# Inverse 47-point DFT of a long convolution: three overlapping products per eight values of m in place of five separate ones

## The chip, the cores and the metric

One core of a Trainium2 chip runs the whole kernel in one launch. The metric is the device time of one execution in microseconds. The kernel before was timed three times; every table below comes from those times and from one further execution that was profiled.

## The reference

The input x has 8 batches of 3008 positions and 256 channels. Each channel of each batch is filtered in the frequency domain, and every resulting position then goes through a two-layer network with a rational activation:

```python
X = np.fft.rfft(x, axis=1)
Y = X * (filt_r + 1j * filt_i)[None, :, :]
y = np.fft.irfft(Y, n=3008, axis=1)            # 8 x 3008 x 256
h = y.reshape(24064, 256) @ w_in               # 2048 columns
P = a[0] + a[1]*h + a[2]*h**2 + a[3]*h**3
Q = 1.0 + np.abs(b[0])*np.abs(h) + np.abs(b[1])*h**2
out = (P / (Q + 1e-6)) @ w_out                 # 24064 x 256
```

## The kernel before

The transform of length 3008 is split as 64 x 47 (a prime-factor split, so that there are no twiddle factors between the two). It has three stages, all on TensorE (PE) in fp32.

*Stage 1* (`stage1`, lines 292 to 306) is the 47-point forward DFT: tiles of 96 rows (48 positions, one of them zero, times two halves of the 64) and 512 columns. A tile is loaded (`stage1_load`), multiplied by `a1_sb` on line 300, copied out by ACT (line 263, through `evac`) and stored to the DRAM scratch `scr1`.

*Stage 2* (`Stage2`, lines 308 to 389) reads `scr1` back with 128 rows (real and imaginary parts of 64 values), does the 64-point forward DFT (line 348), the product with the filter (lines 355, 356, 367, 372), and the 64-point inverse DFT (line 381), and stores the result to the scratch `scr2` (`store`, line 389). The result has one row of `scr2` for each of 24 frequencies k of the 47-point transform (the input is real, so 24 of 47 do), by 128 rows (real or imaginary part r, and m from 0 to 63), by 256 channels.

*Stage 3* (`stage3`, lines 410 to 438) is the inverse 47-point DFT, and turns channels onto partitions for the network. For one pair of values of m (m and m + 32) the data are 96 rows (24 k, two parts r, two halves) by 256 channels. The data are the stationary operand, 128 channels (one half `cc`) at a time, and the constant `e_sb`, 96 x 94, is the moving one: 94 columns are the 47 positions of each of the two m. The 256 pairs are cut into 52 `chunks` of five (the first two are five and one). A chunk is one load `tl` (lines 419 and 420; the first two chunks in two row ranges), and for each `cc` five products side by side in one PSUM bank (line 426). ACT then copies the bank to `xh` as fp32r (line 435), and VectorE (DVE) writes the remainder to `xl` (line 437). `xh` and `xl` are rings of 1536 columns (`RX`), so that a piece across the end of the ring is written in two. In the profile, an fp32 product is two records of weight load (PEld) and matmul (PE); an fp32r product is one.

*The network* works on tiles of 512 positions, 47 in all, each in 16 `Unit`s of 128 hidden columns. A unit has six products into `h_u` (lines 459, 460, 462), a dozen elementwise operations on ACT, DVE and GpSimd (POOL), and six products into the two output banks (lines 536 to 538), issued `LAG` = 4 units later.

*The order.* The instruction order on PE, ACT, DVE and POOL is the order in which the program issues them. `first_batch` (the head, lines 595 to 646) does stages 1 and 2 of batch 0 and the first two chunks of stage 3, beside the unpacking of the weights. `pipeline` (lines 648 to 744) then runs the 752 units, and puts at most one item of convolution work into a unit: either one group of stage 3 (one `cc` of a chunk, two groups to a chunk) or one product of stages 1 and 2 of a later batch (`conv_items`), the latter against a credit of 0.38 per unit. A chunk is begun, with its load, in units 1 and 9 of a tile (`XF`), if the ring has room and the next tile needs it or its batch is ready (lines 689 to 700). All loads and stores of this stage are issued by the SP queue, in order of the program; a load into a buffer waits on SP until its last readers are done. `tl` has two buffers, so chunk k waits for the products of chunk k - 2.

Of the kernel before, what the change touches and what calls it, by code (L numbers as in the profile page):

```python
# [9 lines left out]
F32 = mybir.dt.float32  # L10
# [12 lines left out]
S = 3008  # L23
N1, N2 = 64, 47
NH = 32
K2 = 24
R1 = 96
C = 256
G = 94
GE = 96  # L30
DFF = 2048
LAG = 4
RATES = 0.6, 0.38
# [26 lines left out]
def shape_constants():  # L60
    n2 = np.arange(N2)
    k2 = np.arange(K2)
    th = 2 * np.pi * np.outer(n2, k2) / N2
    a1 = np.zeros((48, 2, K2, 2, 2))
    for h in range(2):
        a1[:N2, h, :, 0, h] = np.cos(th)
        a1[:N2, h, :, 1, h] = -np.sin(th)
    a1 = a1.reshape(R1, R1)

    ph = 2 * np.pi * np.outer(np.arange(N1), np.arange(N1)) / N1  # L70
    co, si = np.cos(ph), np.sin(ph)
    fwd = np.block([[co, -si], [si, co]])
    inv = np.block([[co, si], [-si, co]])

    e = np.zeros((K2, 2, 2, 2, N2))
    w = np.where(k2 == 0, 1.0, 2.0) / S
    for h in range(2):
        e[:, 0, h, h, :] = w[:, None] * np.cos(th.T)
        e[:, 1, h, h, :] = -w[:, None] * np.sin(th.T)
    e = e.reshape(R1, G)  # L80

    k = (N2 * np.arange(N1)[:, None] + N1 * k2[None, :]) % S
    sgn = np.where(k > S // 2, -1.0, 1.0)
    sgn[(k == 0) | (k == S // 2)] = 0.0
    sgn = np.concatenate([sgn, -sgn], 0)
    mats = np.zeros((128, 3, 128))
    mats[:, 0], mats[:, 1], mats[:, 2] = fwd, inv, np.concatenate([inv[64:], inv[:64]])
    small = np.zeros((R1, R1 + GE))
    small[:, :R1], small[:, R1 : R1 + G] = a1, e
    f = lambda v: np.ascontiguousarray(v, dtype=np.float32)  # L90
    return f(mats), f(small), f(sgn)


def index_maps():
# [5 lines left out]


@with_exitstack
def conv_moe(ctx: ExitStack, tc: tile.TileContext, xp, fr, fi, w_in, w_out, ab, mats, small, sgn, outT):
    nc = tc.nc
    B = xp.shape[0]

    consts = ctx.enter_context(tc.tile_pool(name="consts", bufs=1))
    dram = ctx.enter_context(tc.tile_pool(name="dram", bufs=3, space=DRAM))
    conv = ctx.enter_context(tc.tile_pool(name="conv", bufs=2))
# [8 lines left out]
    wo_sb = consts.tile([128, 8, 2, TT], F32R, name="wo_sb")  # L118
    xh = xl = None
    mats_sb = consts.tile([128, 3, 128], F32, name="mats_sb")  # L120
    small_sb = consts.tile([R1, R1 + GE], F32, name="small_sb")
    a1_sb, e_sb = small_sb[:, :R1], small_sb[:, R1 : R1 + G]
    words = consts.tile([128, 128], F32, name="words_sb")
    sgn_sb, ab_sb, abs_sb, cf_sb = words[:, :K2], words[:, 32:44], words[:, 64:76], words[:, 96:120]
    flag_sb = words[:, 120:121].bitcast(I32)
# [3 lines left out]
    col = lambda i, n=1: cf_sb[:, i : i + n]  # L129
# [5 lines left out]
    def load_flag():  # L135


        nc.scalar.activation(abs_sb, ab_sb, AF.Abs)
        sq, c, d, e = col(8, 2), col(10, 2), col(12, 2), col(14)
        tt(out=sq, in0=ab_sb[:, 6:8], in1=ab_sb[:, 6:8], op=ALU.mult)  # L140
        tt(out=c, in0=abs_sb[:, 8:10], in1=abs_sb[:, 10:12], op=ALU.mult)
        stt(out=c, in0=c, scalar=16.0, in1=sq, op0=ALU.mult, op1=ALU.is_ge)
        stt(out=c, in0=abs_sb[:, 10:12], scalar=1e-6, in1=c, op0=ALU.is_ge, op1=ALU.mult)
        stt(out=d, in0=abs_sb[:, 10:12], scalar=2e-6, in1=abs_sb[:, 6:8], op0=ALU.mult, op1=ALU.is_le)
        tt(out=c, in0=c, in1=d, op=ALU.mult)

        stt(out=e, in0=B1, scalar=4.000004, in1=col(9), op0=ALU.mult, op1=ALU.subtract)
        tt(out=e, in0=e, in1=e, op=ALU.mult)
        tt(out=col(9), in0=col(9), in1=col(9), op=ALU.mult)
        stt(out=e, in0=col(9), scalar=1e-10, in1=e, op0=ALU.mult, op1=ALU.is_le)  # L150
        tt(out=col(10), in0=col(10), in1=e, op=ALU.mult)
        tt(out=flag_sb, in0=col(10), in1=col(11), op=ALU.mult)
# [100 lines left out]
        return wo_sb[:, f // 2, k, c : c + 128]  # L253

    scr1 = [dram.tile([K2, 128, C], F32, tag="scr1", name=f"scr1_{b}") for b in range(B)]
    scr2 = [dram.tile([K2, 128, C], F32, tag="scr2", name=f"scr2_{b}") for b in range(B)]

    def rows(scr):
        return scr.rearrange("k (g m) c -> (k g) m c", m=NH)
# [23 lines left out]
    def stage1_load(b, q):  # L283

        tag = "xin" if b or q < XB else ("f1", "f2")[q % 2]
        xin = conv.tile([R1, 2, TT], F32, tag=tag, name=f"xin{b}_{q}", bufs=XB if tag == "xin" else FB)
        nc.sync.dma_start(
            xin.rearrange("p a b -> p (a b)"), xp[b, :, 4 * q : 4 * q + 4, :].rearrange("p m c -> p (m c)")
        )
        return xin  # L290
# [17 lines left out]
    class Stage2:  # L308
# [77 lines left out]
            banks.done(bank, 0.5)  # L386

        def store(self, q):
            nc.sync.dma_start(scr2[self.b][4 * q : 4 * q + 4].rearrange("k p c -> p k c"), self.ev.pop(q))

    def stage2(b):
        s = Stage2(b)
# [12 lines left out]
                s.store(i // 2 - 1)  # L405


    chunks = [(0, 5), (5, 6)] + [(g, min(g + 5, B * NH)) for g in range(6, B * NH, 5)]

    def stage3(k):  # L410

        g0, g1 = chunks[k]
        tl = conv.tile([R1, 5, C], F32, tag="tl", name=f"tl{k}")
        i = g0
        while i < g1:
            b, m = divmod(i, NH)
            n = min(g1, (b + 1) * NH) - i

            for r in (slice(0, 80), slice(80, R1)) if k < 2 else (slice(0, R1),):
                nc.sync.dma_start(tl[r, i - g0 : i - g0 + n], rows(scr2[b])[r, m : m + n, :])  # L420
            i += n
        for cc in range(2):
            yield 1.1
            bank, pt = banks.tile(f"x_{k}_{cc}")
            for i in range(g1 - g0):
                nc.tensor.matmul(  # L426
                    pt[:, i * G : i * G + G], tl[:, i, cc * 128 : cc * 128 + 128], e_sb, start=True, stop=True
                )
            yield

            t0, t1 = g0 * G, g1 * G
            cut = min(t1, (t0 // RX + 1) * RX)
            parts = [(slice(a % RX, a % RX + z - a), pt[:, a - t0 : z - t0]) for a, z in ((t0, cut), (cut, t1)) if a < z]
            for o, p in parts:
                nc.scalar.activation(xh[:, cc, o], p, AF.Copy)
            for o, p in parts:
                v.tensor_tensor(out=xl[:, cc, o], in0=p, in1=xh[:, cc, o].bitcast(F32), op=ALU.subtract)  # L437
            banks.done(bank, 0.5)
# [156 lines left out]
    def first_batch():  # L595

        s = Stage2(0)
        s.more = [xpool.tile([128, 6 - FB, 4, C], F32, tag=x, name=f"f{x}") for x in ("xh", "xl")]
        xin = {}
        fl = iter(range(6))  # L600

        def do(tokens):
            for c in tokens:
                if c == "W":
                    dec.load()
                elif c == "D":
                    dec.step()
                elif c == "F":
                    s.load_filter(next(fl))

        nc.scalar.dma_start(ab_sb, ab.rearrange("(o n) -> o n", o=1).broadcast_to([128, 12]))
        nc.sync.dma_start(small_sb, small)
        for q in range(8):
            xin[q] = stage1_load(0, q)
        do("W")
        nc.scalar.dma_start(sgn_sb, sgn)
        nc.scalar.dma_start(mats_sb, mats)
        load_flag()
        square_scalars()
        for q in range(8):  # L620
            run(stage1(0, q, xin.pop(q)))
            do(HA[q])
        for q in range(XB - 1):
            s.load(q)
        for q in range(2):
            s.double_filter(q)
        do(HM)
        for i in range(12 + ZL):
            if i < 12:
                run(s.product(i))  # L630
            if i >= ZL:
                run(s.inverse(i - ZL))
            q, j = divmod(i, 2)
            if j == 0 and q + XB - 1 < 6:
                s.load(q + XB - 1)
            elif j and q + 2 < 6:
                s.double_filter(q + 2)
            if i > ZL and (i - ZL) % 2:
                s.store((i - ZL) // 2)
            do(HB[i])  # L640
        nonlocal xh, xl
        xh, xl = (xpool.tile([128, 2, RX], F32R, tag=x, name=x) for x in ("xh", "xl"))
        for k in range(2):
            run(stage3(k))
        dec.part(HD)
        assert dec.done == dec.loaded == HD
# [134 lines left out]
def unpermute(outT, nb):  # L781
    seq, _ = index_maps()
    col = np.zeros(S, np.int64)
    col[seq.reshape(2, NH, N2).transpose(1, 0, 2).reshape(-1)] = np.arange(S)
    o = outT.reshape(C, nb, S)[:, :, col]
    return np.ascontiguousarray(o.transpose(1, 2, 0)).reshape(nb * S, C)

# [30 lines left out]
```

## Time and profile before

| what | value |
|---|---|
| median of three runs | 2540.5 us (2538.84 to 2540.68) |
| the profiled execution | 2541.1 us, span 2538.9 us |
| granted TensorE clock, mean | 0.988 |
| PE busy | 2483.7 us (98%) |
| DVE, ACT, POOL busy | 2263.7, 2199.2, 1856.3 us |
| stage 3 on PE, line 426 | 1024 records, 131.5 us busy |
| stage 3 evacuation | 134 instructions each on ACT (59.8 us busy) and DVE (68.2 us) |
| DMA | 208.76 MB, mean 82 GB/s |

The span is the time from the first to the last instruction of the profiled execution; its own time is 2.2 us longer. Records of matmuls overlap, and their ends are modelled, so a group's busy time is the union of its records and not their number times their mean. The time that a record really takes from PE is the distance between the starts of neighbours. A row of the chain of waits gives a start, a length, and the work that occupied that part of the chain; "x10" is ten records in a row.

### The profile page before, as it was taken

Reading aid. Unit: us, or ns where it says so; the run is one execution under the profiler, and the core shown is the slowest. Engines: PE = TensorE matmul, PEld = TensorE weight load, DVE = VectorE, ACT = ScalarE, POOL = GpSimd, SP = SyncE. Lnnn points to the kernel's source line nnn. Section 1 sums busy time; section 2 is a strip of 40 time slices with the busy share of each in tenths; the row PEclk is TensorE's granted clock in tenths of the full one; section 3 lists DMA queues with packets and bytes.
Section 4 is the critical chain, followed back from the end, with each engine's and each line's share of the span. In section 5 each row is a group of like instructions: output and inputs, shape, how many; then the busy total and the mean of one; then the engine's idle time right before and its main releaser. Section 6 shows DMA issues by size and latency. Waiting matters only on the chain.

```text
span 2538.9 us, 35897 instructions
## 1 busy us (share of the span) xinstructions
PE 2483.7 (98%) x10712; PEld 1935.9 (76%) x10712; DVE 2263.7 (89%) x3549; ACT 2199.2 (87%) x4170; POOL 1856.3 (73%) x1984
## 2 busy tenths in 40 slices
PE   5799999999999999999999999999999999999998
PEld 1477777777777777777777777777777778888887
DVE  5779988999889998899888998899988999999998
ACT  4588889888988889888998889988898889999997
POOL 3558876788668876788668886688767887677676
PEclk8799999999999999999999999999999999999999
DMA  8653331332223231232223232233323210000000
GB/s 255 190 140 100 102 116 54 107 97 86 73 76 102 83 97 54 83 110 88 75 60 109 86 97 73 69 97 95 89 62 95 70 52 28 25 25 17 25 9 19
DMA packets 102813, 208.76 MB, mean 82 GB/s; under 512 B 8752, under 2 KB 58512, under 8 KB 102608
## 3 DMA queue, kind: packets, MB, share of 16 engines
q1 hardware_dynamic: 99536, 199.34, 26.6%
q10 hardware_dynamic: 3072, 7.03, 0.9%
q8 instruction: 87, 1.43, 0.2%
q14 instruction: 118, 0.97, 0.1%
HBM read 131.36 MB, written 74.97 MB: 81 GB/s over the span
## 4 chain that ended last, share of the span: by engine, by line
PE 94%; DMA 2%; DVE 2%; ACT 2%; issue 0%; SPq 0%; ACTq 0%; DVEq 0%
PE o L536 13%; PE o L537 13%; PE o L538 13%; PE h_u L459 13%; PE h_u L460 13%; PE h_u L462 13%; PE x L426 4%; PE s L300 4%; PE y L348 3%; PE z L381 3%; DMA scr<-s1e 1%; DMA f<-fi 0%; DMA fxl<-fi 0%; DMA xin<-xp 0%; ACT s1e L263 0%
## 5 line engine op out<-in xcount | busy, mean ns | idle before, releaser
L518 POOL TENSOR_TENSOR q_u<-q_u,hi_u 128x512 f32<-128x512 f32 x752 | 974.5, 1296 | 490.5 <-DVE hi_u L513 472.6
L536 PE MATMUL o<-hi_u,wo_sb 128*128 128x512 f32 x1504 | 701.2, 466 | 0.0
L467 ACT ACTIVATE q_u<-h_u 128x512 f32<-128x512 f32 x752 | 450.3, 599 | 201.3 <-PE h_u L462 144.5
L513 DVE SCALAR_TENSOR_TENSOR hi_u<-h_u,words_sb,a_u 128x512 fp32r<-128x512 f32 x752 | 561.1, 746 | 61.9 <-ACT a_u L489 59.2
L521 DVE SCALAR_TENSOR_TENSOR h_u<-h_u,words_sb,q_u 128x512 f32<-128x512 f32 x752 | 566.5, 753 | 53.8 <-POOL q_u L518 53.4
L459 PE MATMUL h_u<-xh,wi_sb 128*128 128x512 f32 x1504 | 596.9, 397 | 3.7 <-DVE xl L437 3.7
L537 PE MATMUL o<-lo_u,wo_sb 128*128 128x512 f32 x1504 | 589.4, 392 | 0.3 <-DVE lo_u L527 0.3
L538 PE MATMUL o<-hi_u,wo_sb 128*128 128x512 f32 x1504 | 589.1, 392 | 0.0
L460 PE MATMUL h_u<-xl,wi_sb 128*128 128x512 f32 x1504 | 588.2, 391 | 0.0
L499 POOL TENSOR_SCALAR q_u<-q_u,words_sb 128x512 f32<-128x512 f32 x752 | 583.6, 776 | 3.6 <-ACT a_u L484 3.6
L504 DVE SCALAR_TENSOR_TENSOR h_u<-w_u,words_sb,h_u 128x512 f32<-128x512 f32 x752 | 562.7, 748 | 4.3 <-ACT w_u L474 4.3
L527 DVE TENSOR_TENSOR lo_u<-h_u,a_u 128x512 fp32r<-128x512 f32 x752 | 515.8, 686 | 0.1
L484 ACT ACTIVATE a_u<-q_u 128x512 f32<-128x512 f32 x752 | 475.6, 632 | 0.1
L489 ACT ACTIVATE a_u<-a_u 128x512 f32<-128x512 f32 x752 | 471.2, 627 | 0.0
L480 ACT ACTIVATE q_u<-q_u 128x512 f32<-128x512 f32 x752 | 469.6, 624 | 0.0
L462 PE MATMUL h_u<-xh,wi_sb 128*128 128x512 f32 x1504 | 465.2, 391 | 0.0
L474 ACT ACTIVATE w_u<-h_u 128x512 f32<-128x512 f32 x752 | 444.1, 591 | 0.0
L536 PEld LDWEIGHTS o<-hi_u,wo_sb 128*128 128x128 f32 x1504 | 283.1, 188 | 112.9 <-issue 63.6
L537 PEld LDWEIGHTS o<-lo_u,wo_sb 128*128 128x128 f32 x1504 | 283.2, 188 | 110.2 <-issue 60.1
L459 PEld LDWEIGHTS h_u<-xh,wi_sb 128*128 128x128 f32 x1504 | 283.5, 189 | 72.3 <-DVE lo_u L527 4.7
L460 PEld LDWEIGHTS h_u<-xl,wi_sb 128*128 128x128 f32 x1504 | 283.6, 189 | 64.8 <-issue 4.1
L538 PEld LDWEIGHTS o<-hi_u,wo_sb 128*128 128x128 f32 x1504 | 282.5, 188 | 62.2
(96 smaller groups left out, 1889.9 us busy)
## 6 DMA issues: line engine op xcount, KB each, us to landing
xin<-xp SPq DMA_DIRECT2D x64, 384.0 KB, 3.9
scr<-s1e SPq DMA_DIRECT2D x64, 384.0 KB, 4.1
xin<-scr SPq DMA_DIRECT2D x48, 512.0 KB, 4.9
scr<-ev SPq DMA_DIRECT2D x48, 512.0 KB, 4.6
outT<-oe SPq DMA_DIRECT2D x47, 512.0 KB, 3.3
f<-fr SPq DMA_DIRECT2D x87, 256.0 KB, 4.1
f<-fi SPq DMA_DIRECT2D x87, 256.0 KB, 3.8
tl<-scr SPq DMA_DIRECT2D x44, 480.0 KB, 4.1
```

The costliest lines, as they stand in the source:

```text
L459: nc.tensor.matmul(o, w_in_part(0, f, cc), xh[:, cc, ts], start=cc == 0, stop=False)
L460: nc.tensor.matmul(o, w_in_part(0, f, cc), xl[:, cc, ts], start=False, stop=False)
L462: nc.tensor.matmul(o, w_in_part(1, f, cc), xh[:, cc, ts], start=False, stop=cc == 1)
L499: nc.gpsimd.tensor_scalar(out=self.q, in0=self.q, scalar1=AIK, scalar2=SGN, op0=ALU.mult, op1=ALU.add)
L504: v.scalar_tensor_tensor(out=H, in0=w, scalar=PK, in1=H, op0=ALU.add, op1=ALU.mult)
L513: nc.vector.scalar_tensor_tensor(out=self.hi, in0=self.H, scalar=self.p0, in1=self.a, op0=ALU.add, op1=ALU.mult)
L518: nc.gpsimd.tensor_tensor(out=self.q, in0=self.q, in1=self.hi.bitcast(F32), op=ALU.mult)
L521: nc.vector.scalar_tensor_tensor(out=self.H, in0=self.H, scalar=self.p0, in1=self.q, op0=ALU.add, op1=ALU.subtract)
L527: nc.vector.tensor_tensor(out=self.lo, in0=self.H, in1=self.a, op=ALU.mult)
L536: nc.tensor.matmul(o, w_out_part(0, f, dd), self.hi, start=f == 0, stop=False)
L537: nc.tensor.matmul(o, w_out_part(0, f, dd), self.lo, start=False, stop=False)
L538: nc.tensor.matmul(o, w_out_part(1, f, dd), self.hi, start=False, stop=f == 15)
```

## The change

Stage 3 no longer takes one pair of m at a time. `scr2` is laid out as [m, r, k, channel], so that eight neighbouring m are 8 x 2 x 24 = 384 rows in one contiguous piece, which is loaded as three slices of 128 rows. The 384 x 376 matrix that turns them into 8 x 47 = 376 positions is block diagonal with eight blocks of 48 x 47, so a slice of 128 rows touches only the blocks that it overlaps: columns 0 to 141, 94 to 282 and 235 to 376 (`EZ`). Each slice is one product, of 141, 188 and 141 columns, all three into the same bank; where the ranges overlap (94 to 141 and 235 to 282), the second product is added to the first. A chunk is now four pairs' worth (eight m), 376 columns instead of 470, and there are 64 chunks instead of 52, none of which crosses a batch. Each is loaded by one DMA of 384 KB in runs of 1 KB; the two row ranges of the first chunks are gone, and the first two chunks are now as large as the others. A store of stage 2 becomes two DMAs of 64 rows each (r = 0 and 1), in runs of 4 KB. The constants `a1` and `e` are two inputs now: `a1` is loaded first by SP in place of `small`, and `e` (128 x 470) by ACT behind `mats`. The host's order of the output columns follows.

```diff
+EZ = slice(0, 3 * N2), slice(2 * N2, 6 * N2), slice(5 * N2, 8 * N2)
...
-    e = np.zeros((K2, 2, 2, 2, N2))
-    w = np.where(k2 == 0, 1.0, 2.0) / S
-    for h in range(2):
-        e[:, 0, h, h, :] = w[:, None] * np.cos(th.T)
-        e[:, 1, h, h, :] = -w[:, None] * np.sin(th.T)
-    e = e.reshape(R1, G)
+    w = np.where(k2 == 0, 1.0, 2.0)[:, None] / S
+    e = np.kron(np.eye(8), np.concatenate([w * np.cos(th.T), -w * np.sin(th.T)], 0))
+    e = np.concatenate([e[128 * i : 128 * i + 128, z] for i, z in enumerate(EZ)], 1)
...
-    small_sb = consts.tile([R1, R1 + GE], F32, name="small_sb")
-    a1_sb, e_sb = small_sb[:, :R1], small_sb[:, R1 : R1 + G]
+    a1_sb = consts.tile([R1, 128], F32, name="a1_sb")[:, :R1]
+    e_sb = consts.tile([128, 480], F32, name="e_sb")
...
-    scr2 = [dram.tile([K2, 128, C], F32, tag="scr2", name=f"scr2_{b}") for b in range(B)]
+    scr2 = [dram.tile([N1, 2, K2, C], F32, tag="scr2", name=f"scr2_{b}") for b in range(B)]
...
         def store(self, q):
-            nc.sync.dma_start(scr2[self.b][4 * q : 4 * q + 4].rearrange("k p c -> p k c"), self.ev.pop(q))
+            ev = self.ev.pop(q)
+            for r in range(2):
+                nc.sync.dma_start(scr2[self.b][:, r, 4 * q : 4 * q + 4], ev[64 * r : 64 * r + 64])
...
-    chunks = [(0, 5), (5, 6)] + [(g, min(g + 5, B * NH)) for g in range(6, B * NH, 5)]
+    chunks = [(g, g + 4) for g in range(0, B * NH, 4)]
...
         g0, g1 = chunks[k]
-        tl = conv.tile([R1, 5, C], F32, tag="tl", name=f"tl{k}")
-        i = g0
-        while i < g1:
-            b, m = divmod(i, NH)
-            n = min(g1, (b + 1) * NH) - i
-
-            for r in (slice(0, 80), slice(80, R1)) if k < 2 else (slice(0, R1),):
-                nc.sync.dma_start(tl[r, i - g0 : i - g0 + n], rows(scr2[b])[r, m : m + n, :])
-            i += n
+        b, m = divmod(2 * g0, N1)
+        tl = conv.tile([128, 3, C], F32, tag="tl", name=f"tl{k}")
+        rows_ = scr2[b][m : m + 8].rearrange("m r k c -> (m r k) c")
+        nc.sync.dma_start(tl, rows_.rearrange("(a p) c -> p a c", p=128))
         for cc in range(2):
             yield 1.1
             bank, pt = banks.tile(f"x_{k}_{cc}")
-            for i in range(g1 - g0):
+            for a, z in enumerate(EZ):
+                n0 = sum(y.stop - y.start for y in EZ[:a])
                 nc.tensor.matmul(
-                    pt[:, i * G : i * G + G], tl[:, i, cc * 128 : cc * 128 + 128], e_sb, start=True, stop=True
+                    pt[:, z], tl[:, a, cc * 128 : cc * 128 + 128], e_sb[:, n0 : n0 + z.stop - z.start],
+                    start=a == 0, stop=a == 2, skip_group_check=True,
                 )
             yield
...
-        nc.sync.dma_start(small_sb, small)
+        nc.sync.dma_start(a1_sb, a1)
...
         nc.scalar.dma_start(mats_sb, mats)
+        nc.scalar.dma_start(e_sb[:, : e.shape[1]], e)
```

More of the change, by code (lines that the diff above doesn't have):

```diff
@@ L29 @@
 G = 94
-GE = 96
+EZ = slice(0, 3 * N2), slice(2 * N2, 6 * N2), slice(5 * N2, 8 * N2)
 DFF = 2048
@@ L87, in shape_constants @@
     mats[:, 0], mats[:, 1], mats[:, 2] = fwd, inv, np.concatenate([inv[64:], inv[:64]])
-    small = np.zeros((R1, R1 + GE))
-    small[:, :R1], small[:, R1 : R1 + G] = a1, e
     f = lambda v: np.ascontiguousarray(v, dtype=np.float32)
-    return f(mats), f(small), f(sgn)
+    return f(mats), f(a1), f(e), f(sgn)
 def index_maps():
@@ L102, in conv_moe @@
 @with_exitstack
-def conv_moe(ctx: ExitStack, tc: tile.TileContext, xp, fr, fi, w_in, w_out, ab, mats, small, sgn, outT):
+def conv_moe(ctx: ExitStack, tc: tile.TileContext, xp, fr, fi, w_in, w_out, ab, mats, a1, e, sgn, outT):
     nc = tc.nc
@@ L783, in unpermute @@
     col = np.zeros(S, np.int64)
-    col[seq.reshape(2, NH, N2).transpose(1, 0, 2).reshape(-1)] = np.arange(S)
+    col[seq.reshape(-1)] = np.arange(S)
     o = outT.reshape(C, nb, S)[:, :, col]
@@ L797 @@
     xp, fr, fi = layouts(x, filt_r, filt_i)
-    mats, small, sgn = shape_constants()
+    mats, a1, e, sgn = shape_constants()
     ins = {
@@ L806 @@
         "mats": mats,
-        "small": small,
+        "a1": a1,
+        "e": e,
         "sgn": sgn,
```

## The prediction

> **What bounds the kernel now.** I read the page first, then busy time by stage, the PE timeline of a quiet stretch, the chain of waits at both ends of the head, and the waits of the SP queue.
>
> ```profile
> span 2538.9 us, 35897 instructions
> ...
> PE 2483.7 (98%) x10712; PEld 1935.9 (76%) x10712; DVE 2263.7 (89%) x3549; ACT 2199.2 (87%) x4170; POOL 1856.3 (73%) x1984
> ...
> PE 94%; DMA 2%; DVE 2%; ACT 2%; issue 0%; SPq 0%; ACTq 0%; DVEq 0%
> PE o L536 13%; PE o L537 13%; PE o L538 13%; PE h_u L459 13%; PE h_u L460 13%; PE h_u L462 13%; PE x L426 4%; PE s L300 4%; PE y L348 3%; PE z L381 3%; DMA scr<-s1e 1%; DMA f<-fi 0%; DMA fxl<-fi 0%; DMA xin<-xp 0%; ACT s1e L263 0%
> ```
>
> PE is 94% of the chain that ended last, and line 426, the one that changes, is 4% of it. By stage (columns: stretch, its length, busy time of PE, PEld, DVE, ACT, POOL, then granted clock, DMA share, GB/s):
>
> ```profile
> 0.00:97.00 97.00, 55.12 (x105) 21.16 (x105) 63.57 (x134) 42.78 (x67) 41.69 (x52) 0.85 0.83 242
> 97.00:130.00 33.00, 28.04 (x91) 21.34 (x92) 21.20 (x34) 21.29 (x40) 14.06 (x13) 0.63 0.60 168
> 1200.00:1800.00 600.00, 600.00 (x2606) 468.75 (x2605) 540.34 (x839) 527.68 (x1005) 453.53 (x492) 1.00 0.29 85
> ```
>
> Two regimes, then. Up to about 130 us the DMA engines carry 242 GB/s and PE waits; after that PE is full at full clock (600 of 600 us). There, what PE is spared the kernel is spared, and what PE gets on top it pays. So the price of one inverse group on PE decides. The timeline of PE (start, length, line, records), only the rows that mark units:
>
> ```profile
> 1001.31 0.39 PE L536 MATMUL o<-hi_u,wo_sb 128*128 128x512 f32 x1
> ...
> 1004.03 1.02 PE L300 MATMUL s<-xin,small_sb 96*96 96x512 f32 x2
> ...
> 1010.36 1.02 PE L300 MATMUL s<-xin,small_sb 96*96 96x512 f32 x2
> ...
> 1020.29 1.25 PE L426 MATMUL x<-small_sb,tl 96*128 96x94 f32 x10
> ...
> 1024.17 1.25 PE L426 MATMUL x<-small_sb,tl 96*128 96x94 f32 x10
> ...
> 1028.04 1.02 PE L300 MATMUL s<-xin,small_sb 96*96 96x512 f32 x2
> ```
>
> A unit of the MLP without extra work takes 1004.03 - 1001.31 = 2.72 us. From one inverse group to the next there is one unit and one group: 3.87 or 3.88 us, so a group (five products, two records each) adds 1.155 us. From 1004.03 to 1010.36 there are two units and one forward group: 6.33 - 5.44 = 0.89 us for one fp32 product of 512 columns.
>
> **What limits a short record.**
>
> ```profile
> 148.13 1.09 PE x L426 x10
> ...
> 155.88 0.86 PE s L300 x2
> ...
> 205.61 0.86 PE y L348 x2
> ```
> ```profile
> L426 PEld LDWEIGHTS x<-small_sb,tl x1024: 186/192/333, 96.9 to 2423.8; 96*128 96x128 f32 x171
> L426 PE MATMUL x<-small_sb,tl x1024: 244/275/495, 96.9 to 2423.9; 96*128 96x94 f32 x171
> ```
> ```profile
> L300 PEld LDWEIGHTS s<-xin,small_sb x256: 159/163/285, 7.5 to 1924.1; 96*96 96x96 f32 x128
> ```
>
> The chain gives two 512-column records 0.86 us: 0.43 each, 0.84 ns per column. At that rate 94 columns stream in 0.079 us, but the records come every (1.25 - 0.244) / 9 = 0.112 us. Something other than streaming sets their pace, and the loads of stationary data fit: a load of 128 columns takes 192 ns, one of 96 columns 163, so 29 ns for 32 columns, 0.9 ns per column; 128 columns hold the load path for about 0.116 us. That is my reading of 0.112: the load of the next record takes longer than the 94 columns that should hide it. Streaming would need about 133 columns to hide it.
>
> **The change, part by part.**
>
> *Products.* A group (one half cc of a chunk) of five products of 94 columns, for five pairs of m, becomes one of three products of 141, 188 and 141 columns, for four pairs; each product is still two records. All three are longer than 133, so I price them by streaming: 0.118, 0.158, 0.118 us. A group is then 2 x (0.118 + 0.158 + 0.118) = 0.788 us. Before, ten records at 0.112 were 1.12 of the 1.155 us that the group added; the same 0.035 of entry and exit makes 0.823. For hand-overs of a few ns per record I take 0.84. Contraction over 128 rows in place of 96 costs nothing: y on line 348 contracts over 128, s on line 300 over 96, and both take 0.86. Bounds: 0.82 below; above, 0.90, if a load exposes another 13 ns in each record.
>
> The count: 1024 records less the 24 of the head are 100 groups in the stage where PE is full. After, 64 chunks less 2 are 62, with two groups each: 124. So 100 x 1.155 = 115.5 us become 124 x 0.84 = 104.2: **-11.3 us** (-13.8 to -3.9).
>
> Here a rule of the Trainium skill speaks against the whole picture. TensorE: Matmul & The Clock Gate, section Part 3, says that a weight load overlaps matmuls in flight only when they use other row groups of the array. By it no load here would hide, and 128 rows leave no group free at all. The row disagrees: y's two records with 128 rows take the same 0.86 as s's with 96, and 0.112 is less than 0.079 + 0.116.
>
> *Evacuation.* Fewer columns per instruction, more instructions: 52 chunks x 2 + 2 x 15 ring borders (1536 columns) = 134 before, 64 x 2 + 30 = 158 after, with the same columns in all.
>
> ```profile
> L437 DVE TENSOR_TENSOR xl<-x,xh x134: 167/638/650, 100.0 to 2424.8; 128x470 fp32r<-128x470 f32 x72, 128x94 fp32r<-128x94 f32 x2, 128x32 fp32r<-128x32 f32 x2, 128x438 fp32r<-128x438 f32 x2
> ```
> ```profile
> L435 ACT ACTIVATE xh<-x x134: 177/563/598, 99.4 to 2424.2; 128x470 fp32r<-128x470 f32 x72, 128x94 fp32r<-128x94 f32 x2, 128x32 fp32r<-128x32 f32 x2, 128x438 fp32r<-128x438 f32 x2
> ```
>
> The shortest pieces, 167 and 177 ns, bound the fixed cost of one more instruction: at most 24 x 0.167 = 4 us on DVE and 4.2 on ACT, beside 275 and 340 us that they idle (2538.9 - 2263.7, 2538.9 - 2199.2). I cost it at nothing; without that cover it is 4 us.
>
> *Order of the units.* The planner (lines 689 to 740) starts a chunk only in units 1 and 9 of a tile. I replayed its conditions with both lists. Items take 404 units instead of 380 of 752, at most one per unit as before; no group of forward work is forced; nearly all chunks are finished 12 or 13 units before their tile, the tightest, at tile 5, 5 units before it in both. So no stall follows from the order.
>
> *SP queue.* A chunk's load waits until PE has read the buffer of the chunk before the last, and everything behind it on SP waits too:
>
> ```profile
> SPq L420 <- PE x L426: 634.9, 44, 38.9
> ...
> SPq L420 <- DMA scr<-ev: 24.7, 8, 4.4
> ```
> ```profile
> L389 SPq DMA_DIRECT2D scr<-ev x48: 359/382/1379, 58.5 to 2104.8; - x48
> ```
> ```profile
> scr<-ev SPq DMA_DIRECT2D x48, 512.0 KB, 4.6
> ...
> tl<-scr SPq DMA_DIRECT2D x44, 480.0 KB, 4.1
> ...
> tl<-scr SPq DMA_DIRECT2D x3, 384.0 KB, 3.5
> ```
>
> Behind it stand the stores, the filter and input loads of the next batch, and the outputs. In the replay the load leaves at least 13 units (35 us) after the end of that earlier chunk, where before it was 14. A transfer lands in 3.5 to 4.6 us. 48 more stores and 4 more loads (64 for the 60 of before) at 0.38 us of issue are 20 us of SP, spread over 2400. The two halves of a store write runs of 4 KB instead of 1 KB, and the loads read 1 KB runs instead of 5 KB; both lie far ahead of their readers in this stage. Cost nothing; bound 0 to +2.
>
> *The head.* Here nothing hides:
>
> ```profile
> 90.83 3.09 DMA scr<-ev
> ...
> 93.94 2.85 DMA tl<-scr
> ...
> 96.92 4.56 PE x L426 x20
> ...
> 101.89 6.65 DMA xin<-xp
> ...
> 108.68 1.08 PE s L300 x2
> ...
> 118.83 2.09 PE x L426 x10
> ```
> ```profile
> 96.92 5.40 PE L426 MATMUL x<-small_sb,tl 96*128 96x94 f32 x24 [6.86 <-DMA tl<-scr]
> 102.26 0.80 PE L459 MATMUL h_u<-xh,wi_sb 128*128 128x512 f32 x1
> ...
> 108.68 1.07 PE L300 MATMUL s<-xin,small_sb 96*96 96x512 f32 x2 [0.65 <-DMA xin<-xp]
> ```
>
> Before, 80 of the 96 rows of a chunk were loaded ahead of the last store; only 16 rows were left behind it (2.85 us). After, all 384 KB come behind it (3.5 us by the row above), and the second half of the store is issued 0.4 us later: the products start 1.0 us later. The clock is at 0.63 in this stretch, and 24 records at 0.112 would be 2.7 us but took 5.4: the products run at half speed. So four groups of 1.576 us are 6.3 us for 5.4, and the first unit starts at 97.9 + 6.3 = 104.2 for 102.3. Part of this comes back. The forward product s waited 0.65 us for xin, whose load stands on SP behind a chunk load that waits for chunk 0; chunk 0 is now done at 97.9 + 3.15 = 101.1 for 101.5, so that wait is gone: from 102.26 to 108.68 less 0.65 are 5.8 us of work, and s starts at 110.0, 1.3 late. The next group, 2.09 us long at that clock, takes 1.58: 0.5 less. That leaves +0.8. At the start, ACT issues one more transfer, e, ahead of the flag work:
>
> ```profile
> 2.16 0.45 ACTq L617 DMA_DIRECT2D mats_sb<-mats  x1
> 2.64 1.28 ACT L138 ACT_TABLE_LOAD   x1 [2.64 <-issue]
> 4.39 0.21 ACT L138 ACTIVATE words_sb<-words_sb 128x12 f32<-128x12 f32 x1 [0.46 <-DMA words_sb<-ab]
> ```
>
> Its 0.45 us fall into the 0.46 of waiting for ab. Its 240 KB (36 KB less in a1) are 0.8 us of a stage at 242 GB/s, if all of it is late. I take **+1.5 us** for the head (the 0.8 of the products, and most of the 0.8 of the transfer), between -1 (the stores land a microsecond sooner in longer runs, e costs nothing) and +5 (nothing overlaps, and e delays the first stores as well).
>
> **Sum.** The profiled execution took 2541.1 us, 2.2 more than its span, and 0.6 above the median of 2540.5. 2541.1 - 11.3 + 1.5 = 2531.3; less 0.6, 2530.7: **2531**. All lower bounds at once give 2526, all upper ones 2541.
>
> **The rivals.** 0.2% is 5 us, about what a measurement can tell: the borders are 2535.4 and 2545.6.
>
> *A fixed cost in every record* (slower). If the 33 ns between 0.079 and 0.112 are not a load but paid by each record, the new ones take 0.151, 0.191, 0.151, a group 0.986 + 0.035 = 1.021, all groups 126.6 us: +11.1 + 1.5, **2553**. It decides from 0.93 us per group (115.5 / 124). For it: no fp32 record between 94 and 512 columns exists in this trace. Against: a 512-column record would have to stream at 0.78 ns per column. 8%.
>
> *No overlap of loads with 128 short rows* (slower). Should a load not hide behind these products, a group is 2 x (0.394 + 3 x 0.116) + 0.035 = 1.52 us 124 of them 188.5 us instead of 115.5, and with the head the time is about 2615. Against: y and s above, and the 0.112. 2%. This is what the rule of the Trainium skill quoted above would make of the new products.
>
> *The gain goes to new waits* (same). The seven later batches each begin a chunk with a load behind two stores instead of one; the replay leaves 5 units between them and the reader at worst. If a wait of 0.5 to 1 us got through at each, or the head lost its 5 us, 2535 to 2540: about **2538**. Against: SP waited 24.7 us for stores 8 times and PE is still full. 10%.
>
> *Forecast*: 80%, of which 3 lie above 2535.4, at its upper bounds. Hence faster 0.77, same 0.13, slower 0.10. The range 2525 to 2540 holds nearly all of the forecast and half of the third rival; the 10% on the slower side stay out.
>
> **What would show it.** In the profile after: 768 records on the product's line, of which 124 groups of six take about 0.80 us on the chain; x units near 3.56 us; PE still 600 of 600 us in the middle. Right for the head: products starting near 98 us. Wrong if a group exceeds 0.93 us, if PE shows gaps beside chunk loads after 130 us, or if DVE passes PE on the chain.

## The result, and the profile after

The changed kernel takes 2567.36 us (median of four runs, 2564.67 to 2567.53) against 2539.67 us of the kernel before: a ratio of 1.0105, interval 1.0092 to 1.0118. It is 1% slower. The forecast was 2531 us, 0.4% below the 2540.5 that it started from. The profiled execution has a span of 2565.6 us. The same views again, first the page (rows as before):

```profile
span 2565.6 us, 35506 instructions
...
PE 2505.1 (98%) x10456; PEld 1924.3 (75%) x10456; DVE 2270.7 (89%) x3573; ACT 2204.0 (86%) x4194; POOL 1856.8 (72%) x1984
...
PE 91%; DVE 3%; DMA 2%; POOL 1%; issue 1%; ACT 1%; SPq 0%; ACTq 0%; DVEq 0%; POOLq 0%
```

PE is still the chain, and still looks full in the middle of the run (stretch, length, busy PE, PEld, DVE, ACT, POOL, clock, DMA share, GB/s):

```profile
1200.00:1800.00 600.00, 599.49 (x2525) 462.30 (x2524) 533.98 (x834) 522.87 (x1000) 446.44 (x483) 1.00 0.28 83
```

The same 600 us, full and at full clock, held 2606 PE records before and hold 2525 now. Part of that is the new shape (six records for ten): the changed kernel with the padding that is described below holds 2549. The rest is seen where nothing was changed. Of the changed kernel, the timeline of PE, one unit of the network near the end, where there is no convolution work left (the first row of each layer and the first of the next unit are enough):

```profile
2470.23 0.40 PE L533 MATMUL o<-hi_u,wo_sb 128*128 128x512 f32 x1
...
2471.63 0.40 PE L456 MATMUL h_u<-xh,wi_sb 128*128 128x512 f32 x1
...
2473.03 0.40 PE L533 MATMUL o<-hi_u,wo_sb 128*128 128x512 f32 x1
```

Before, the same place:

```profile
2467.57 0.39 PE L536 MATMUL o<-hi_u,wo_sb 128*128 128x512 f32 x1
...
2468.93 0.39 PE L459 MATMUL h_u<-xh,wi_sb 128*128 128x512 f32 x1
...
2470.29 0.39 PE L536 MATMUL o<-hi_u,wo_sb 128*128 128x512 f32 x1
```

Six products of the second layer took 2468.93 - 2467.57 = 1.36 us, 0.227 each; they take 1.40 now, 0.233 each, and the first layer's six do the same. A unit went from 2.72 to 2.80 us. Its instructions had not changed, and no wait or idle time stands in these rows: each product simply takes 3% longer. The new groups, on the chain of waits (start, length, what), cost what was forecast:

```profile
388.30 0.86 PE s L296 x2
391.94 0.80 PE x L422 x6
395.53 0.80 PE x L422 x6
399.12 0.86 PE s L296 x2
```

0.80 us for six records (0.788 worked out), 3.59 us from one group to the next (3.56 forecast). The head came out close too:

```profile
90.81 4.03 DMA scr<-ev
...
94.91 2.93 DMA tl<-scr
...
97.89 3.52 PE x L422 x12
...
101.83 6.74 DMA xin<-xp
...
108.70 1.97 PE s L296 x2
```

The products start at 97.89 (97.9 forecast), but by two errors that cancel: the last store took 4.03 us where 3.49 were worked out (3.09 and 0.4), and the load 2.93 where 3.5 were. Chunk 0 is done at 101.4 (101.1). The forward product s came at 108.70, where it came before, and not at 110.0: the granted clock between 97 and 130 us was 0.77, against 0.63 before, so the units ahead of it were done sooner, and it waited for xin after all.

### The profile page after: what moved, and what is told of

The parts are those of the page before. It is cut to its first block, busy times and chain, and to the rows that moved or that the text cites. A ratio compares the mean times of both kernels' runs of the same rounds, so it can differ in the third digit from the quotient of the medians.

```text
span 2565.6 us, 35506 instructions
## 1 busy us (share of the span) xinstructions
PE 2505.1 (98%) x10456; PEld 1924.3 (75%) x10456; DVE 2270.7 (89%) x3573; ACT 2204.0 (86%) x4194; POOL 1856.8 (72%) x1984
## 3 DMA queue, kind: packets, MB, share of 16 engines
q8 instruction: 85, 1.39, 0.2%
## 4 chain that ended last, share of the span: by engine, by line
PE 91%; DVE 3%; DMA 2%; POOL 1%; issue 1%; ACT 1%; SPq 0%; ACTq 0%; DVEq 0%; POOLq 0%
PE h_u L456 13%; PE h_u L459 13%; PE o L534 13%; PE h_u L457 13%; PE o L535 13%; PE o L533 13%; PE x L422 4%; PE s L296 4%; PE y L344 3%; PE z L377 3%; DVE h_u L518 1%; DMA scr<-s1e 1%; DVE hi_u L510 1%; POOL q_u L515 0%; DVE h_u L501 0%
## 5 line engine op out<-in xcount | busy, mean ns | idle before, releaser
L456 PE MATMUL h_u<-xh,wi_sb 128*128 128x512 f32 x1504 | 606.2, 403 | 3.6 <-DVE xl L434 3.1
L459 PE MATMUL h_u<-xh,wi_sb 128*128 128x512 f32 x1504 | 471.7, 394 | 0.0
L533 PEld LDWEIGHTS o<-hi_u,wo_sb 128*128 128x128 f32 x1504 | 282.7, 188 | 114.4 <-issue 63.6
L456 PEld LDWEIGHTS h_u<-xh,wi_sb 128*128 128x128 f32 x1504 | 284.1, 189 | 81.1 <-DVE lo_u L524 6.5
L459 PEld LDWEIGHTS h_u<-xh,wi_sb 128*128 128x128 f32 x1504 | 283.1, 188 | 67.1
```

What stands on the lines that cost most here:

```text
L456: nc.tensor.matmul(o, w_in_part(0, f, cc), xh[:, cc, ts], start=cc == 0, stop=False)
L459: nc.tensor.matmul(o, w_in_part(1, f, cc), xh[:, cc, ts], start=False, stop=cc == 1)
L533: nc.tensor.matmul(o, w_out_part(0, f, dd), self.hi, start=f == 0, stop=False)
```

## The experiments

The puzzle was a product that nobody had touched. What the change did move was memory: the new constants `a1_sb` and `e_sb` take 2432 bytes per partition where `small_sb` took 768, and the two `tl` buffers 4096 bytes each (they share their place with other tiles of that size) where they took 5120. From the program's allocation, `xh`, `xl`, `hi_u` and `lo_u`, the moving operands of the network's products, so start 384 bytes earlier. The weights `wi_sb` and `wo_sb` lie in front of all this and stayed. The distance from weights to moving operands can be worked out from the tiles' widths: weights and constants together take 65536 + 1536 + 768 + 512 = 68352 bytes of a partition before, 267 times 256, and 70016 now, which leaves 128 over; the tiles between are multiples of 256 bytes. Theory A is that the place decides; theory B, the rival, that the new work itself slows the units.

**Placement put back; the old kernel misplaced.** Two edits of one number each. In the changed kernel:

```diff
-    e_sb = consts.tile([128, 480], F32, name="e_sb")
+    e_sb = consts.tile([128, 576], F32, name="e_sb")
```

> The changed kernel with 384 unused bytes per partition behind e, which puts every tile behind it (xh, xl, hi_u, lo_u, the elementwise tiles) at the addresses they had before the change. Theory A (place: an fp32r product takes longer when its moving operand starts at another offset in SBUF; the operands moved by 384 bytes, from 384 to 0 modulo 512): a unit without extra work falls from 2.79 to 2.72 us, a group of the inverse still adds 0.80 us, and the time is about 2531 us, the predicted one. Theory B (work: the new products, transfers or order slow the units themselves, through PE's queue, SBUF traffic or the clock): units stay at 2.79 and the time at 2567. Theory C (any shift of addresses gives an arbitrary outcome, not a matter of the offset modulo 512): something else, with the same addresses as before still likely 2.72.

Measured: 2532.95 us, ratio 0.9977 to the kernel before (0.9967 to 0.9986). This version is called the padded kernel below. In the kernel before:

```diff
-    small_sb = consts.tile([R1, R1 + GE], F32, name="small_sb")
+    small_sb = consts.tile([R1, R1 + GE + 32], F32, name="small_sb")
...
-        nc.sync.dma_start(small_sb, small)
+        nc.sync.dma_start(small_sb[:, : R1 + GE], small)
```

> The kernel before, all of its work unchanged, with 128 unused bytes per partition behind its small constants: the same tiles now start at 0 modulo 512, as in the changed kernel. Theory A: units without extra work rise from 2.72 to 2.79 us and the time to about 2580 us (the units next to extra work were already somewhat above 2.72, so less than 752 x 0.074 = 55 us is added). Theory B: 2.72 and 2540 us, no change.

Measured: 2575.07 us, ratio 1.0145 (1.0128 to 1.0162). The timeline of PE near the end, one unit, of the changed kernel with its padding:

```profile
2466.91 0.39 PE L456 MATMUL h_u<-xh,wi_sb 128*128 128x512 f32 x1
...
2468.27 0.39 PE L533 MATMUL o<-hi_u,wo_sb 128*128 128x512 f32 x1
```

And of the kernel before with its own:

```profile
2466.91 0.40 PE L459 MATMUL h_u<-xh,wi_sb 128*128 128x512 f32 x1
...
2468.31 0.40 PE L536 MATMUL o<-hi_u,wo_sb 128*128 128x512 f32 x1
```

1.36 us with the changed kernel, 1.40 with the kernel before: the time went over with the place. Theory B is refuted: the kernel before has none of the new work, and its units are slow at this place. 96 unused columns take 34 us out of the changed kernel, and 32 unused columns put 36 us into the old one (2575.07 - 2538.82, timed together).

**Which places.** Padding of 128 and 256 bytes behind `e` (512 and 544 columns), and later one of 64 (496 columns).

> The changed kernel with 128 unused bytes behind e: the moving operands start at 128 modulo 512, like the weights. Theory A leaves open which offsets are dear; if the cost comes from moving operand and weights at equal or different offsets, this place differs from both 2.72 and 2.79, or equals one of them. If only the parity of 128-byte steps counts, it goes with the offset 384 (2.72 us, some 2531 us). Theory B: 2.79 and 2567.

> The changed kernel with 256 unused bytes behind e: the moving operands start at 256 modulo 512. If only the parity of 128-byte steps counts (Theory A), it goes with the offset 0: 2.79 us per unit and 2567 us. If only the offset 384 is cheap, the same, and the run with 128 bytes is dear too. Theory B: 2.79 and 2567.

> The changed kernel with 64 unused bytes behind e: the moving operands start at 64 modulo 256, the weights at 128. If the cost goes with equality of the 128-byte half in which the two start, 64 lies in the other half than 128: dear, 2.79 us per unit and 2567 us. If any offset other than the opposite one is cheap, or the effect is graded, something between 2.72 and 2.79 us and 2533 and 2567.

Measured: 2535.50, 2566.71 and 2572.68 us, one run each. 128 and 384 modulo 512 are cheap, 0, 256 and 64 are dear. So it is a matter of 256 bytes, and 64 goes with 0, not with 128.

**Which operand.** On the cheap placement, gaps of 128 bytes: one in the pool of hi and lo (with another in the pool of x, which brings x back to 128 modulo 256), or one in the pool of x alone.

```diff
+        xpool.tile([128, 32], F32, tag="gapx", name="gapx")
         s.more = [xpool.tile([128, 6 - FB, 4, C], F32, tag=x, name=f"f{x}") for x in ("xh", "xl")]
...
+        mlp.tile([128, 32], F32, tag="gap", name="gap")
         dec.part(HD)
```

> The changed kernel with 384 bytes of padding (the cheap placement), but only hi_u and lo_u, the moving operands of the second layer, move by 128 bytes to 0 modulo 256; xh and xl stay at 128 modulo 256, the weights and the elementwise tiles a, q, w where they were. Moving-operand theory: the second layer's products rise from 227 to about 233 ns each and the first layer's stay at 227; a unit without extra work takes about 2.757 us and the whole about 2550 us. Elementwise theory (the dear place comes from ACT, DVE and POOL reading and writing a, q and w beside PE): all products stay at 227 ns, 2.72 us and 2533.

> The mirror of the run before: only xh and xl, the moving operands of the first layer, move by 128 bytes to 0 modulo 256. Moving-operand theory: the first layer's products rise to about 233 ns, the second layer's stay at 227; 2.757 us per unit and about 2550 us. If the writes of hi_u and lo_u by DVE mattered and not the reads by PE, this run stays at 2.72 us and 2533. Elementwise theory: 2.72 and 2533.

Measured: 2554.92 and 2550.62 us. With only hi and lo moved, the timeline of PE near the end (first row of the second layer, of the first layer, and so on):

```profile
2468.70 0.39 PE L456 MATMUL h_u<-xh,wi_sb 128*128 128x512 f32 x1
...
2470.07 0.40 PE L533 MATMUL o<-hi_u,wo_sb 128*128 128x512 f32 x1
...
2471.47 0.39 PE L456 MATMUL h_u<-xh,wi_sb 128*128 128x512 f32 x1
```

With only x moved:

```profile
2466.65 0.40 PE L456 MATMUL h_u<-xh,wi_sb 128*128 128x512 f32 x1
...
2468.04 0.39 PE L533 MATMUL o<-hi_u,wo_sb 128*128 128x512 f32 x1
...
2469.42 0.40 PE L456 MATMUL h_u<-xh,wi_sb 128*128 128x512 f32 x1
```

In the first, the first layer takes 1.37 us and the second, whose operand moved, 1.40. In the second, the first layer, whose operand moved, takes 1.39 and the second 1.38. The layer whose operand moved is the dearer one each time, but the other is not back at 1.36. The starts of all products in the units without extra work (about 290 units in each trace) show where the rest sits. With only hi and lo moved, the six products of the first layer take 0.231, 0.233, 0.231, 0.228, 0.227 and 0.227 us in turn, on average, and those of the second between 0.226 and 0.237 to the end. With only x moved, the six of the second layer take 0.231, 0.231, 0.230, 0.227, 0.227 and 0.227. So each layer pays for its own operand, and the price runs on into the first three or four products of the next layer; the clean split that was expected (2.72 plus 0.04 all in one layer) is not seen. Why it runs on is not shown. What both runs do refute is the elementwise tiles as the cause: a, q and w did not move, and both runs are dear, 22.0 and 17.7 us above the 2532.95 of the cheap placement.

**Alone, or against the weights.** A gap of 128 bytes ahead of the weights, with the padding behind `e` kept at 576 columns (everything moves) or cut to 544 (only weights and small constants move).

```diff
+    consts.tile([128, 32], F32, name="gap")
     wi_sb = consts.tile([128, 4, 2, 2, TT], F32R, name="wi_sb")
```

> The cheap placement with 128 bytes of padding ahead of the weights as well, so that everything, weights included, moves by 128: weights and moving operands are both at 0 modulo 256. Relative theory (it counts whether weights and moving operand lie at the same offset modulo 256, say because the next load and the running product read alternately): cheap, 2.72 us and 2533. Absolute theory (only the moving operand's own offset counts): dear, 2.79 us and 2567.

> Only the weights of both layers (and the small constants) move by 128 bytes to 0 modulo 256; the moving operands and all other tiles stay at the cheap place, 128 modulo 256. Relative theory: dear, 2.79 us and 2567. Absolute theory: cheap, 2.72 us and 2533.

Measured: 2530.72 and 2569.60 us. The timeline of PE near the end, with all moved (the gap is one more line of the program, so line numbers are one higher):

```profile
2466.87 0.39 PE L457 MATMUL h_u<-xh,wi_sb 128*128 128x512 f32 x1
...
2468.23 0.39 PE L534 MATMUL o<-hi_u,wo_sb 128*128 128x512 f32 x1
...
2469.59 0.39 PE L457 MATMUL h_u<-xh,wi_sb 128*128 128x512 f32 x1
```

With the weights alone moved:

```profile
2467.99 0.40 PE L457 MATMUL h_u<-xh,wi_sb 128*128 128x512 f32 x1
...
2469.39 0.40 PE L534 MATMUL o<-hi_u,wo_sb 128*128 128x512 f32 x1
...
2470.79 0.40 PE L457 MATMUL h_u<-xh,wi_sb 128*128 128x512 f32 x1
```

A unit takes 2.72 us in the first and 2.80 in the second. With all moved, the moving operands lie at 0 modulo 256, the dear place of the changed kernel, and are cheap; with the weights alone moved, they lie at the cheap place and are dear. The absolute theory is wrong, the relative one holds. The other engines are cleared too: in these units PE alone reads the weights, and moving them is enough. All placements together (start within a partition modulo 256, and the median unit without extra work; the first four times are medians of four or more runs, the others one run each):

| kernel | weights | xh, xl | hi, lo | unit, us | time, us |
|---|---|---|---|---|---|
| before | 128 | 128 | 128 | 2.72 | 2539.67 |
| changed | 128 | 0 | 0 | 2.79 | 2567.36 |
| changed, 384 bytes | 128 | 128 | 128 | 2.72 | 2532.95 |
| before, 128 bytes | 128 | 0 | 0 | 2.79 | 2575.07 |
| changed, 128 bytes | 128 | 128 | 128 | 2.72 | 2535.50 |
| changed, 256 bytes | 128 | 0 | 0 | 2.79 | 2566.71 |
| changed, hi and lo moved | 128 | 128 | 0 | 2.77 | 2554.92 |
| changed, x moved | 128 | 0 | 128 | 2.77 | 2550.62 |
| changed, all moved | 0 | 0 | 0 | 2.72 | 2530.72 |
| changed, weights moved | 0 | 128 | 128 | 2.79 | 2569.60 |
| changed, 64 bytes | 128 | 64 | 64 | 2.80 | 2572.68 |

Timed over several runs, the kernel with all moved:

> The placement with everything moved by 128 bytes, weights too, timed: by the relative theory it is the cheap placement again, 2531 to 2534 us, and the best version so far against the kernel before (2538.8 to 2540.5): a ratio of 0.997 to 0.998. The absolute theory, already against the single run, would give 2567.

Measured: 2530.22 us, ratio 0.9961 (0.9947 to 0.9975). It is faster than the kernel before and than the changed one, as is one more version below (2530.36).

**What is still missing.** At the cheap placement the change brings 5.9 us (2538.82 - 2532.95), where 9.8 were forecast. The traces tell the head from the units. From the first product of the 21st unit to that of the last unit, the kernel before takes 2336.9 us (183.74 to 2520.61) and the padded one 2330.3 (182.82 to 2513.15): 6.6 less, where 118 groups at 0.83 us in place of 94 at 1.155 would give 10.6. So about 4 us are lost in the units. The head scatters by as much: with all moved the 21st unit starts at 179.60 us, with 128 bytes of padding at 185.00, though both do the same work there as the padded kernel. The 2.7 us by which the kernel with all moved (2530.22) lies below the padded one stand there too: from the 21st unit to the last it needs 2330.8 us, no less than the padded one. What differs in the head was not separated. In the units of the padded kernel PE's loads wait longer for DVE's `lo_u`, the last reader of a bank that the next unit needs. The waits (who for whom: us in total, times, longest) before:

```profile
PEld h_u L459 <- DVE lo_u L527: 4.7, 14, 0.6
```

and in the changed kernel with 384 bytes:

```profile
PEld h_u L456 <- DVE lo_u L524: 12.4, 25, 1.1
```

One part of the change alone on the kernel before, the smaller chunks with the old products:

```diff
-    chunks = [(0, 5), (5, 6)] + [(g, min(g + 5, B * NH)) for g in range(6, B * NH, 5)]
+    chunks = [(g, g + 4) for g in range(0, B * NH, 4)]
```

> The kernel before with one part of the change alone: chunks of four pairs in place of five (64 instead of 52), with the old 94-column products, loads and scratch. PE's work is nearly the same (124 groups of 8 records at 0.112 + 0.035 = 0.931 us are 115.4 us, against 115.5). If the larger number of groups, loads and evacuations costs nothing by itself, 2540 us and loads waiting some 5 us for lo_u; if it is what makes DVE late in the changed kernel, 2543 to 2545 us and waits of about 12 us.

Measured: 2544.38 us, ratio 1.0021 (1.0011 to 1.0031), and:

```profile
PEld h_u L459 <- DVE lo_u L527: 9.6, 22, 1.0
```

So the larger number of groups costs about 4 us by itself (3 to 8 by the interval), without any shorter product. In its trace they stand in the units: 2341.6 us from the 21st unit to the last, 4.7 more than before. And the changed kernel at the cheap placement with DVE's 47 output copies given to ACT:

```diff
-EV1, EV2, EVO = "A", "AV", "AV"
+EV1, EV2, EVO = "A", "AV", "AA"
```

> The changed kernel at the cheap placement, with the 47 output copies of DVE (0.74 us each) moved to ACT. Of the 11.3 us that I forecast from the products, about 4 are missing in the cheap placement, and PE's loads wait 12.4 us for DVE's lo_u where they waited 4.7 before. Theory D (DVE falls behind in the now shorter units with inverse groups, and PE pays): DVE has 35 us less to do, the waits of the loads for lo_u fall to some 5 us, and the time falls by 2 to 4 us, to about 2530. Rival (the waits stem from order, not from DVE's load, or ACT becomes the late one): same as the cheap placement, 2533, or slower.

Measured: 2530.36 us, ratio 0.9964 (0.9952 to 0.9976). The waits:

```profile
PEld h_u L456 <- DVE lo_u L524: 10.6, 22, 1.1
```

The time fell by 2.6 us as expected, but the waits only to 10.6, not to 5. Against the padded kernel's trace the units take 2.0 us less (2328.3 us from the 21st to the last) and the end behind the start of the last unit, where the last copy goes out, 1.2 us less, while the head is 1.3 us later. So DVE's load is part of what is missing; the rest is perhaps where a group's remainder `xl` stands in DVE's order, behind ACT's `xh`. No run separated it, but DVE's waits in the padded kernel fit:

```profile
DVE xl L434 <- ACT xh L432: 88.6, 93, 3.5
```

## Why the prediction was wrong, point by point

**The step that failed** is one that the sum did not have. It priced the split of the constants as a transfer only (240 KB in the head), and took the 752 units at 2.72 us as given. The new constant tile moved every tile behind it, the moving operands of all 9024 fp32r products among them, from the same place modulo 256 bytes as their weights to one 128 bytes off, and each then took 0.233 us for 0.227. The price is 2567.36 - 2532.95 = 34.4 us, less than 752 x 0.07 = 53, because units with a group in them lose less. The chain of waits of the padded kernel (start, length, what):

```profile
469.93 0.80 PE x L422 x6
...
473.48 0.80 PE x L422 x6
```

From one group to the next it is 3.55 us here, and 3.59 in the changed kernel: 0.04 of difference where a unit without a group shows 0.07. The starts in the trace say why these units lose only half: in the padded kernel too, the products behind a group are not at 0.227 us at once. The second to fifth take 0.236, 0.228, 0.232 and 0.231 (medians over 118 groups), together as long as in the changed kernel, and only the next ones 0.227. No view of a profile that was read for "PE is full" could have warned of this; the start addresses in the program's own allocation would have said that the operands move, though not what that costs, and the prediction did not ask for them.

**Products: right.** A group is 0.80 us on the chain, against 0.788 worked out, and adds 0.83 to a unit in the padded kernel (3.55 - 2.72), against 0.84 taken. The price by streaming holds at 141 and 188 columns: in that trace the next record of a group starts 0.119 to 0.123 us after one of 141 columns and 0.158 to 0.163 after one of 188, for 0.118 and 0.158 worked out. The rival of a fixed cost per record (1.02 us per group) is refuted, and with it 2553. That it was the load that held 94 columns at 0.112 us stays an argument; no run tested it.

**No overlap of loads: refuted.** The rule of the Trainium skill, TensorE: Matmul & The Clock Gate, Part 3, would have made it 1.5 us with 128 rows. It is 0.80.

**Evacuation and order: mis-sized.** I cost the larger number of groups at nothing, and at 4 us without cover. It cost about 4 us (2544.38 for 2539.96), and PE's loads waited 9.6 us for DVE instead of 4.7. The idle time of DVE that was to cover it did not: in the padded kernel a third of it, 88.6 of 264.5 us, is DVE waiting for ACT's copy ahead of a group's own remainder. This is the third rival, gain lost to new waits, with about its size (3.5 to 7 us forecast) and its place wrong: not the loads behind two stores, but `lo_u` on DVE.

**SP queue: right.** No wait of PE for a chunk's load stands in the changed kernel behind the head.

**Head: within its bounds, by luck.** The start of the products was met by two errors that cancel, in the store and in the load. The start of s differs by 0.02 us from before, not by the 1.3 worked out, again by two: the first units ran faster than I took them, and the wait for xin did not go away. In the padded kernel, whose head does the same work, s is 1.2 us late. The +1.5 us of the sum is smaller than the scatter of the heads (the 21st unit starts between 179.60 and 185.00 us), and no run tests it.

**Sum.** With the place repaired, 2532.95 lies in the forecast range, 2 us above the 2531. Against the kernel before as timed beside it (2538.82) 3.9 of the 9.8 us are missing, in the term that evacuation was denied. Two statements of the sum do not add up. All upper bounds at once are 2540.5 - 3.9 + 5 = 2541.6, and 2547.6 with the 2 us of the SP queue and the 4 of evacuation that it names itself; it gives 2541. And the range to 2540 holds all of the third rival (2535 to 2540), not half. Neither reaches 2567.

## What to carry to other kernels

When an edit changes the size of any tile, list the start addresses of the operands of the hottest instruction before and after, and keep them as they were with padding; otherwise a change of layout is measured together with the change that was meant. After any change, compare first the distance between starts of instructions that were not changed: a busy share of 100% says nothing of how long each one takes.

## What the runs showed of the hardware that was not expected

An fp32r product of 128 x 128 by 512 columns, in a row of such products with alternating weights, took 0.227 us when weights and moving operand started at the same place modulo 256 bytes of their partitions (both at 128, or both at 0), and 0.233 when they did not (weights and operand at 128 and 0, 0 and 128, 128 and 64). Whether the same half of 256 bytes would be enough, or the places must be equal, no run tells: two unequal places in one half were not tried. After a change of layer the old price held for three or four products. The fp32 groups of the inverse show no such step: 0.80 us on the chain at either place of the changed kernel. The Trainium skill, TensorE: Matmul & The Clock Gate, section "Step-by-step: what each phase is for", states that weights and the streamed operand are read through two independent ports, so that a load takes nothing from the running product. A price that depends on where the two start relative to each other (2530.72 and 2569.60 us for the same program with everything moved, or the weights alone) is not what two independent readers would give. Whether load and product do get in each other's way, or something else does, was not separated; steps finer than 64 bytes were not tried.
